# Two token blocks share the weight groups of the first MLP, and the weight steps are spread out

## The chip, the cores and the metric

The kernel runs on one core of one Trainium2 chip. The metric is device time in microseconds (us) of one execution. The engines are TensorE (PE in the profile, with its weight loads as PEld), VectorE (DVE), ScalarE (ACT), GpSimd (POOL) and SyncE (SP), whose queue issues all the DMAs here. A write "out<-in" in a row of the profile names the tiles that an instruction writes and reads; L785 is line 785 of the kernel before.

## The reference

Three layers in a row, float32 in and out, 4 batches of 576 tokens, 8 heads of 64:

```python
# 1 attention, with a decay by f
scores = scale * q @ k.T + (cum[:, None] - cum[None, :])    # cum = cumsum(log f), causal mask
attn = exp(scores - max) / (sum + 1e-9);  x = attn @ v      # -> x (2304, 512)
# 2 first MLP, w_in (512, 2048), w_out (2048, 512)
h = x @ w_in;  g = h * tanh(softplus(h));  x = g @ w_out
# 3 second MLP, w_in (512, 1024), w_out (1024, 512)
h = x @ w_in;  s = h * softmax(h);  z = layernorm(s) * g_ln;  out = z @ w_out
```

The weights come as float64 values.

## The kernel before

**Precision.** TensorE works on fp16 here. Each float32 operand is split into a high and a low fp16 half under a power-of-two scale, and each product is three matmuls (high·high, high·low, low·high).

**Attention** makes x in chunks of 128 tokens (64 in one chunk of each batch), in "slots" of four, two or one heads: 30 slots to a batch. A slot's scores go into one of three PSUM tiles `sp` (L436, L437, L441 on the PE). `step_r` takes the maximum on the DVE (L483; for a chunk of 64 tokens L493, L496 and L497) and the exponential on ACT (L485, or L499 and L500). `step_h` casts the high half (L523, ACT), subtracts for the low half (L524, POOL) and transposes both by a DMA on the SP queue (`pT`, L529). Three slots later L555 to L557 multiply by v. `fin` scales the chunk (L566 to L574) and transposes it by DMA (L582) into `xT`, blocks of 256 tokens, in three buffers.

**The weights of the first MLP** come in 16 parts of 1 MB, in four groups: group g holds two parts of w_in (`wi_r`) and two of w_out (`wo_r`), which serve the hidden tiles fi = 4g to 4g+3 of 128 channels. `load` (L121) issues a part's DMA on the SP queue into one of two buffers. `conv` (L130) turns float64 bits into float32 with three DVE steps (L137, L139, L141) and issues eight small matmuls (`gram`, L160), from which `bound` derives the scale of a group (L175 to L180, L329). `split` makes the halves, on ACT and POOL (L201, L203, L206) or on ACT and DVE (L198, L199). All these steps stand in one list, `wsteps`, and `wgo(n)` emits the next n. During the first slots WS0 = 3 are emitted a slot, and later WS1 = 4 in each half step of the loop below.

**The first MLP** goes block by block (j, nine blocks), in units of one fi: unit n is block n // 16, fi n % 16. `up` (L775) makes h for a pair of units in PSUM, 12 matmuls each (L785). `mish_a`, `mish_b` and `mish_c` make g (L797, L798 on ACT; L802 and L806 on DVE; L803 to L805 and L811 on ACT; L812 on POOL). `down` (L818) multiplies by w_out, 12 matmuls to a unit (L829). Block 0 closes its sum after each group of four fi and adds it, with the group's own scale `rho`, to `acc` in SBUF (L838 and L840 on the DVE), since the later groups' scales are not known yet; the other blocks sum all 16 fi in PSUM. `evac` (L847) hands the block to the second MLP, whose work (L1028, L1068) begins when attention is done.

**The order.** One loop of half steps (L906 to L954) writes the program: it emits the weight steps that a unit needs, and paces the attention slots through `att_slots` (L890), with EB = 190 half steps for all of them, a lower bound from the next block's need and an upper bound from the three `xT` buffers. A scheduler then fixes each engine's order from this program, so an engine's order can differ from the order of the lines.

Of the kernel before, what the change touches and what calls it, by code (L numbers as in the profile page):

```python
# [8 lines left out]
F32 = mybir.dt.float32  # L9
F16 = mybir.dt.float16  # L10
# [8 lines left out]
P = 128  # L19
# [18 lines left out]
R0 = 9  # L38
GRP = [4, 2, 1, 1, 1]
WS0 = 3  # L40
WS1 = 4
WPF = 2
S2P = 1
EB = 190
# [164 lines left out]
def emit(tc, q, k, v, f, w_in, w_out, w2_in, w2_out, g_ln, out):  # L209
# [580 lines left out]
    def mish_a(p):  # L790
        j, fi = divmod(2 * p, NF1)
        ph = hps.pop(p)
        ta = mp.tile([P, 2, TB], F32, tag="ta", name=f"ta_{p}")
        th = mp.tile([P, 2, TB], F32, tag="th", name=f"th_{p}")
        tmp[p] = (ta, th)
        for b, a, e in segs(j):
            nc.scalar.activation(ta[:, :, a:e], ph[:, :, a:e], AF.Exp, scale=usc(b, fi // 4))  # L797
        nc.scalar.activation(th, ph, AF.Copy, scale=ths[:, fi // 4:fi // 4 + 1] if j else -0.4 * HSC)  # L798

    def mish_b(p):  # L800
        ta, th = tmp[p]
# [16 lines left out]
    def down(n):  # L818
        j, fi = divmod(n, NF1)
        gt = gts[n // 2]  # L820
        if n % 2:
            del gts[n // 2]
        first, last = (fi % 4 == 0, fi % 4 == 3) if j == 0 else (fi == 0, fi == NF1 - 1)
        for t in range(TT):
            if first:
                x2ps[j, t] = psx.tile([P, DM], F32, tag=f"x2_{t}", name=f"x2_{j}_{t}_{fi}")
            o = x2ps[j, t]
            for m, (lg, lw) in enumerate(((0, 0), (0, 1), (1, 0))):
                nc.tensor.matmul(  # L829
                    o, gt[:, lg, n % 2, t * P:(t + 1) * P], wout[:, fi, lw * 512:(lw + 1) * 512],  # L830
                    start=(first and m == 0), stop=(last and m == 2))
        if last and j == 0:
            for t in range(TT):
                o = x2ps.pop((0, t))
                g = fi // 4
                if g == 0:
                    acc[t] = mp.tile([P, DM], F32, tag="acc", name=f"acc{t}")
                    nc.vector.tensor_scalar(acc[t], o, rho[:, g:g + 1], None, op0=ALU.mult)  # L838
                else:
                    nc.vector.scalar_tensor_tensor(acc[t], o, rho[:, g:g + 1], acc[t], op0=ALU.mult, op1=ALU.add)  # L840
                if g == 3:
                    x2ps[0, t] = acc[t]
        if fi == NF1 - 1:
            for t in range(TT):
                evac(j, t)

    def evac(j, t):  # L847
# [12 lines left out]
        for p0 in (0, 64):  # L860
            b = (tt * P + p0) // S
            if p0 and b == (tt * P) // S:
                continue
            if j == 0:
                if t == 0:
# [5 lines left out]
            nc.vector.scalar_tensor_tensor(  # L871
                us2[p0:, tt:tt + 1], m[p0:, 1:2], 2.0 ** -14, (kb[b] if j else kbz)[p0:], op0=ALU.mult, op1=ALU.mult)

    need = []
    for j in range(NBLK):
# [14 lines left out]
    def att_slots(n):  # L890
# [11 lines left out]
    wq = {}  # L902
    done = {"d": 0}
    st2 = None

    for hn in range(2 * (NF + 5)):  # L906
# [2 lines left out]
        att_now = live and pos["k"] < att_slots(hn)  # L909
        if att_now:  # L910
            slot_pre()
        if half == 0:
            if n % 2 == 0 and 0 <= n // 2 - 1 < NF // 2:
                mish_b(n // 2 - 1)
            if att_now:
                slot_mid()
            if live:
                while n < NF1 and (w1_split, n // 4 * 2 + 1) not in wdone:
                    wgo(1)
                up(n)  # L920
        else:
            if live and n % 2:
                while n > NF1 and wsteps:
                    wgo(1)
                mish_a(n // 2)
            if n % 2 == 0 and 0 <= n // 2 - 1 < NF // 2:
                mish_c(n // 2 - 1)
            if att_now:
                slot_mid()
            tgt = n - 2 if (n > DL + 8 or n >= NF) else n - DL  # L930
            while done["d"] < min(tgt, NF):
                if done["d"] // 2 not in gts:
                    break
                while done["d"] < NF1 and (w2_split, done["d"] // 2) not in wdone:
                    wgo(1)
                down(done["d"])
                done["d"] += 1
        if att_now:
            slot_pe()
# [180 lines left out]
```

## Time and profile before

| | us |
|---|---|
| median of 3 runs (lowest to highest) | 859.61 (858.01 to 860.01) |
| the profiled execution's own span, first to last instruction | 856.0 |
| busy in it: PE, DVE, ACT, POOL | 739.0, 617.6, 548.2, 440.8 |

The median stands 3.6 us above the span of the profiled execution; that is what lies around the span, plus the difference between runs. Busy time of matmuls is modelled where they are pipelined, so a PE that reads as 95% busy may be full. The profile's "PEclk" is the share of full TensorE speed that was granted. The share of the whole span hides that the stages differ: up to about 140 us the weights are still being converted, from then to about 500 us attention and the first MLP run together, and from 600 us on the chain of work that ended last is matmuls alone.

### The profile page before, as it was taken

What the parts mean: (1) busy time and instruction counts of PE and PEld (TensorE: products, weight loads), DVE (VectorE), ACT (ScalarE), POOL (GpSimd) and SP (SyncE); (2) the same over time, 40 slices, a digit from 0 to 9 for tenths busy, and PEclk for the clock granted to TensorE, in tenths of its full rate; (3) what the DMA queues carried; (4) which work ended last, traced back from release to release, by engine and by line L of the source; (5) the groups of instructions that cost most, each with busy time, mean ns of one, the idle gap of its engine ahead of it and who ended that gap; (6) DMA issues with size and microseconds to landing.
All of it is one profiled execution on the core that took longest, in us unless ns stands there. A gap on an engine that the chain in (4) does not pass through costs nothing.

```text
span 856.0 us, 15746 instructions
## 1 busy us (share of the span) xinstructions
PE 739.0 (86%) x5822; PEld 456.4 (53%) x5822; DVE 617.6 (72%) x1158; ACT 548.2 (64%) x1202; POOL 440.8 (51%) x341
## 2 busy tenths in 40 slices
PE   0545776689999999997999999986999999999998
PEld 0334543447656666575666767553555554444443
DVE  6799999498867989769896755599566444665551
ACT  5645647868779877877877767686855554333331
POOL 2268676755976667755678653128832222022110
PEclk9999997889999999999999999999999999999999
DMA  9999555477899898988897533941013323344443
GB/s 239 229 215 281 160 176 94 93 137 145 153 174 190 168 169 153 184 155 153 173 180 119 115 70 63 233 156 61 26 38 87 74 64 73 87 101 106 104 88 82
DMA packets 328568, 114.83 MB, mean 134 GB/s; under 512 B 317676, under 2 KB 317676, under 8 KB 328492
## 3 DMA queue, kind: packets, MB, share of 16 engines
q1 hardware_dynamic: 328492, 113.84, 63.9%
q8 instruction: 45, 0.74, 0.4%
q14 instruction: 31, 0.25, 0.1%
HBM read 46.59 MB, written 9.55 MB: 66 GB/s over the span
## 4 chain that ended last, share of the span: by engine, by line
PE 37%; DVE 24%; DMA 12%; ACT 11%; issue 8%; POOL 6%; SPq 1%; DVEq 0%; ACTq 0%; POOLq 0%
PE h L1028 11%; PE o L1068 10%; PE x L829 7%; PE h L785 6%; DMA pT<-ph 3%; POOL ph L524 3%; DVE th L806 2%; DVE ta L802 2%; ACT p L485 2%; DVE ph L521 1%; DMA w2i_r<-in_moe_w_in_dram 1%; DMA ktr<-kn 1%; DMA rawk<-in_k_dram 1%; ACT p L500 1%; DVE nm L483 1%
## 5 line engine op out<-in xcount | busy, mean ns | idle before, releaser
L829 PE MATMUL x<-wout,gt 128*128 128x512 f16 x864 | 219.8, 387 | 18.2 <-ACT gt L811 8.8
L785 PE MATMUL h<-xT,win 128*128 128x256 f16 x1728 | 221.2, 277 | 2.3 <-POOL win L203 1.7
L524 POOL TENSOR_TENSOR ph<-p,ph 128x512 f16<-128x512 f32 (+4 forms) x120 | 157.0, 1314 | 81.3 <-ACT ph L523 35.0
L785 PEld LDWEIGHTS <-win 128*128 128x128 f16 x1728 | 168.5, 100 | 45.8 <-POOL win L203 1.8
L812 POOL TENSOR_TENSOR gt<-th,gt 128x512 f16<-128x512 f32 x72 | 92.4, 1284 | 106.5 <-ACT gt L811 105.3
L829 PEld LDWEIGHTS <-gt 128*128 128x128 f16 x864 | 80.0, 100 | 99.3 <-ACT gt L811 11.6
L1056 POOL TENSOR_TENSOR z<-sl,z 128x1024 f16<-128x1024 f32 x18 | 38.7, 2151 | 138.0 <-DVE s2c L1035 111.1
L1028 PE MATMUL h<-w,x2T 128*128 128x512 f16 x432 | 98.4, 380 | 2.9 <-POOL w L206 1.6
L1068 PE MATMUL o<-wo,zT 128*128 128x512 f16 x432 | 96.5, 379 | 0.5 <-DMA zT<-z 0.5
L555 PE MATMUL pv<-vt,pT 128*128 128x64 f16 (+3 forms) x480 | 71.4, 203 | 23.0 <-DMA pT<-ph 20.2
L806 DVE SCALAR_TENSOR_TENSOR th<-ta,th 128x512 f32<-128x512 f32 x72 | 71.9, 1000 | 24.7 <-ACT ta L805 24.4
L485 ACT ACTIVATE p<-sp,nm 64x64 f32<-64x64 f32 (+7 forms) x128 | 61.3, 484 | 38.7 <-DVE nm L483 21.1
L436 PE MATMUL sp<-ktr,qa 128*128 128x64 f16 (+6 forms) x304 | 59.6, 253 | 22.8 <-ACT p L485 8.7
L811 ACT CAST gt<-th 128x512 f16<-128x512 f32 x72 | 44.3, 615 | 50.2 <-DVE th L806 49.9
L802 DVE TENSOR_SCALAR ta<-ta 128x512 f32<-128x512 f32 x72 | 58.8, 816 | 20.4 <-ACT ta L797 19.9
L1028 PEld LDWEIGHTS <-x2T 128*128 128x128 f16 x432 | 42.3, 98 | 53.9 <-issue 4.0
L555 PEld LDWEIGHTS <-pT 128*128 128x128 f16 (+3 forms) x480 | 45.4, 101 | 47.9 <-DMA pT<-ph 31.3
L556 PE MATMUL pv<-vt,pT 128*128 128x64 f16 (+3 forms) x480 | 70.4, 198 | 0.6 <-DVE vt L199 0.6
L557 PE MATMUL pv<-vt,pT 128*128 128x64 f16 (+3 forms) x480 | 70.2, 198 | 0.0
L1068 PEld LDWEIGHTS <-zT 128*128 128x128 f16 x432 | 42.2, 98 | 51.5 <-DMA zT<-z 1.0
L437 PE MATMUL sp<-ktr,qb 67*128 67x64 f16 (+6 forms) x304 | 63.3, 254 | 3.6 <-DVE qb L401 3.6
L1039 ACT ACTIVATE e<-h,s2c 128x1024 f32<-128x1024 f32 x18 | 21.7, 1204 | 68.1 <-DVE s2c L1037 68.1
(235 smaller groups left out, 1443.5 us busy)
## 6 DMA issues: line engine op xcount, KB each, us to landing
wi_r<-in_moe_w_in_dram SPq DMA_DIRECT2D x8, 1024.0 KB
wo_r<-in_moe_w_out_dram SPq DMA_DIRECT2D x8, 1024.0 KB
rawk<-in_k_dram SPq DMA_DIRECT2D x25, 256.0 KB
rawv<-in_v_dram SPq DMA_DIRECT2D x25, 256.0 KB
x2d<-x2h SPq DMA_DIRECT2D x18, 256.0 KB
out_dram<-ro SPq DMA_DIRECT2D x18, 256.0 KB
w2i_r<-in_moe_w_in_dram SPq DMA_DIRECT2D x4, 1024.0 KB
w2o_r<-in_moe_w_out_dram SPq DMA_DIRECT2D x4, 1024.0 KB
```

The lines of the kernel that those rows point to most:

```text
L485: nc.scalar.activation(pv[:m, g * (i + 1) * P + off:g * (i + 1) * P + end], s3[:, g, off:end], AF.Exp, bias=nm[:m, g:g + 1], accum_out=rs[ ...
L524: nc.gpsimd.tensor_tensor(p4[:, :, 1], pv3, p4[:, :, 0], op=ALU.subtract)
L555: nc.tensor.matmul(o, pT[a0:a1, k, :m], vh, start=(c == 0), stop=False)
L556: nc.tensor.matmul(o, pT[a0:a1, k, :m], vl, start=False, stop=False)
L557: nc.tensor.matmul(o, pT[a0:a1, k + 1, :m], vh, start=False, stop=(c == i))
L785: nc.tensor.matmul(ph, win[:, (fi // 4) * NC1 + c, col:col + P], x[:, lx * NC1 + c, :], start=(m == 0), stop=(m == 3 * NC1 - 1))
L802: nc.vector.tensor_scalar(ta, ta, E20, 1.0, op0=ALU.min, op1=ALU.add)
L806: nc.vector.scalar_tensor_tensor(th, ta, 2.5, th, op0=ALU.subtract, op1=ALU.mult)
L812: nc.gpsimd.tensor_tensor(gt[:, 1], th, gt[:, 0], op=ALU.subtract)
L829: nc.tensor.matmul(o, gt[:, lg, n % 2, t * P:(t + 1) * P], wout[:, fi, lw * 512:(lw + 1) * 512], start=(first and m == 0), stop=(last and ...
L1028: nc.tensor.matmul(h[:, half * 512:(half + 1) * 512], x[:, lx * NC1 + c, :], self.w2[:, half * NC1 + c, lw * 512:(lw + 1) * 512], start=(n ...
L1068: nc.tensor.matmul(o, zT[:, lz * NF2 + c, :], self.wo[:, c, lw * 512:(lw + 1) * 512], start=(n == 0), stop=(n == 3 * NF2 - 1))
```

## The change

- The order of units is a list: block 0's groups 0 (fi 0 to 3) and 1, then block 1's group 0, block 0's group 2, block 1's group 1, and so on, block 1 one group behind; from unit 28 on it is as before. So the first 32 units are 0–3, 4–7, 16–19, 8–11, 20–23, 12–15, 24–27, 28–31.
- Blocks 0 and 1 (j < NR = 2) both close their sums after each group. Block 1's `acc` lies in the third `xT` buffer, and its scales take the form that block 0's had (a constant at L798, `kbz` at L871).
- Weight steps are forced only by a unit that needs them; WS1 goes from 4 to 1 a half step.
- Until unit 15 is emitted, attention may not pass slot 32 (of 120).
- `across` (L329), which borrows a score tile of PSUM for a scale's sum, picks one that no pending score holds.

```diff
-WS1 = 4
+WS1 = 1
+NR = 2
...
-            k = seq[min(pos["k"], len(seq) - 1)]
-            t = sps[cnt["s"] % (len(sps) if k[1] < NCH - 1 else 2)]
-            cnt["s"] += 1
+            k = [seq[min(max(pos["k"] - x, 0), len(seq) - 1)][1] for x in range(2)]
+            held = [x[3].name for y, x in pend.items() if y[0] == "s"]
+            free = [x for x in sps[:len(sps) if max(k) < NCH - 1 else 2] if x.name not in held]
+            t = free[cnt["s"] % len(free)]
...
-        first, last = (fi % 4 == 0, fi % 4 == 3) if j == 0 else (fi == 0, fi == NF1 - 1)
+        first, last = (fi % 4 == 0, fi % 4 == 3) if j < NR else (fi == 0, fi == NF1 - 1)
...
                 if g == 0:
-                    acc[t] = mp.tile([P, DM], F32, tag="acc", name=f"acc{t}")
-                    nc.vector.tensor_scalar(acc[t], o, rho[:, g:g + 1], None, op0=ALU.mult)
+                    if j == 0:
+                        acc[j, t] = mp.tile([P, DM], F32, tag="acc", name=f"acc{t}")
+                    elif t == 0:
+                        w = mlpx.tile([P, 2 * NC1, TB], F16, tag="xT", name=f"xT_acc{j}", bufs=XB)
...
+                    nc.vector.tensor_scalar(acc[j, t], o, rho[:, g:g + 1], None, op0=ALU.mult)
...
         hi = need[j + XB] - 1 if j + XB < NBLK else len(seq) + LAG
+        if n < 2 * units.index(NF1 - 1):
+            hi = min(hi, sum(H // g for g in GRP) + LAG - 1)
...
+    units = list(range(0, 4))
+    for g in range(1, 4):
+        units += list(range(4 * g, 4 * g + 4)) + list(range(NF1 + 4 * g - 4, NF1 + 4 * g))
+    units += list(range(NF1 + 12, NF))
...
-                while n < NF1 and (w1_split, n // 4 * 2 + 1) not in wdone:
+                while u < NR * NF1 and (w1_split, u % NF1 // 4 * 2 + 1) not in wdone:
                     wgo(1)
-                up(n)
+                up(u)
```

What this moves on three engines follows; the lines of the changed kernel are one or two higher up to L830 and eight or nine higher up to L960.

**DVE around the end of the last group's conversions** (`wi_r7`, `wo_r6` are weight parts as they came; `nm_0_3_7` is the negative maximum of batch 0, chunk 3, head 7; `x2_0_0_4` is block 0's sum of group 1). Before, from the last step of `wi_r7` to the first of `wo_r6`:

```order
L141 SCALAR_TENSOR_TENSOR win_93<-wi_r7_758,win_93 128x1024
L179 RECIPROCAL wo_b_159<-wo_b_159 128x1
L628 TENSOR_TENSOR rho_90<-wpt_83,wo_b_159 128x1
L567 TENSOR_SCALAR rr_0_2_1071<-rsum_0_2_591 128x8
L180 TENSOR_SCALAR wo_b_159<-wo_b_159 128x1
L568 RECIPROCAL rr_0_2_1071<-rr_0_2_1071 128x8
L137 TENSOR_SCALAR wout_94<-wo_r6_820 128x1024
```

Now, the same stretch:

```order
L142 SCALAR_TENSOR_TENSOR win_93<-wi_r7_975,win_93 128x1024
L848 SCALAR_TENSOR_TENSOR acc0_1223<-x2_0_0_4_1340,rho_90,acc0_1223 128x512
L569 TENSOR_SCALAR rr_0_3_1387<-rsum_0_3_888 128x8
L848 SCALAR_TENSOR_TENSOR acc1_1225<-x2_0_1_4_1344,rho_90,acc1_1225 128x512
L570 RECIPROCAL rr_0_3_1387<-rr_0_3_1387 128x8
L495 TENSOR_REDUCE ne_0_1289<-sp2_149 64x8
L200 SCALAR_TENSOR_TENSOR wout_94<-wout_94,wo_b_159 128x2x512
L498 TENSOR_REDUCE nm_0_4_0_1288<-sp0_147 64x1
L498 TENSOR_REDUCE nm_0_4_1_1327<-sp1_148 64x1
L176 TENSOR_REDUCE wi_b_158<-gram_151 128x1
L499 TENSOR_TENSOR nm_0_4_0_1288<-nm_0_4_0_1288,ne_0_1289 64x1
L138 TENSOR_SCALAR wout_94<-wo_r6_1159 128x1024
```

Two of block 0's sums, the end of chunk 3, the first two heads of chunk 4 and a split stand there now; the heads 0 to 7 of chunk 3 stand further ahead, two of them directly before `wi_r7`.

**SP queue around the last weight loads** (`rawk`, `rawv`, `rawq` are loads of attention's inputs, `pT` the transposes of its probabilities, `qa` of its queries). Before:

```order
L124 DMA wo_r5_689<-in_moe_w_out_dram 128x2x512
L302 DMA rawk_1_3_1266<-in_k_dram 128x8x64
L124 DMA wi_r6_745<-in_moe_w_in_dram 128x2x512
L124 DMA wi_r7_758<-in_moe_w_in_dram 128x2x512
L124 DMA wo_r6_820<-in_moe_w_out_dram 128x2x512
L398 DMA_TRANSPOSE qa_0_4_1184<-qn_0_4_1180 128x8x64
L124 DMA wo_r7_870<-in_moe_w_out_dram 128x2x512
```

Now:

```order
L303 DMA rawq_1_0_1601<-in_q_dram 64x8x64
L303 DMA rawk_1_0_1603<-in_k_dram 64x8x64
L531 DMA_TRANSPOSE pT_0_3_0_930<-ph_0_3_0_892 128x16x128
L125 DMA wi_r7_975<-in_moe_w_in_dram 128x2x512
L303 DMA rawv_1_0_1605<-in_v_dram 64x8x64
L531 DMA_TRANSPOSE pT_0_3_2_1025<-ph_0_3_2_985 128x16x128
L531 DMA_TRANSPOSE pT_0_3_4_1120<-ph_0_3_4_1075 128x16x128
L125 DMA wo_r6_1159<-in_moe_w_out_dram 128x2x512
L531 DMA_TRANSPOSE pT_0_3_6_1215<-ph_0_3_6_1169 128x16x128
L125 DMA wo_r7_1285<-in_moe_w_out_dram 128x2x512
L531 DMA_TRANSPOSE pT_0_4_0_1338<-ph_0_4_0_1295 128x20x64
```

The load of `wi_r7` stands behind the transpose `pT_0_3_0`, and those of `wo_r6` and `wo_r7` behind three more of chunk 3, where before no transpose of probabilities stood between `wi_r6` and `wo_r7`.

**ACT after the last group's conversions** (`ta_9`, `th_9` belong to block 1's fi 2 and 3, `ta_4` to block 0's fi 8 and 9). Now:

```order
L502 ACTIVATE p32_1_130,rsum_0_4_1287<-sp1_148,nm_0_4_3_1618 64x512
L501 ACTIVATE p32_0_129,rsum_0_4_1287<-sp2_149,nm_0_4_4_1704 64x64
L502 ACTIVATE p32_0_129,rsum_0_4_1287<-sp0_147,nm_0_4_4_1704 64x512
L805 ACTIVATE ta_9_1540<-ta_9_1540 128x512
L202 ACTIVATE rawk_1_2_2161<-rawk_1_2_2161,scu_1_1357 128x512
L813 CAST gt_8_1512<-th_8_1472 128x512
L799 ACTIVATE ta_4_1607<-h_0_8_1557,usc1_0_79 128x512
```

Block 1's first pairs stand ahead of block 0's pair 4, which before stood ahead of chunk 3's exponentials, as here:

```order
L797 ACTIVATE ta_5_1541<-h_0_10_1505,usc1_0_79 128x512
L798 ACTIVATE th_5_1542<-h_0_10_1505 128x512
L198 ACTIVATE wout_94<-wout_94,wo_b_159 128x2x512
L811 CAST gt_4_1518<-th_4_1490 128x512
L803 ACTIVATE ta_5_1541<-ta_5_1541 128x512
L804 ACTIVATE ta_5_1541<-ta_5_1541,c_k1_72 128x512
L805 ACTIVATE ta_5_1541<-ta_5_1541 128x512
L485 ACTIVATE p32_0_129,rsum_0_3_1005<-sp0_147,nm_0_3_0_1006 128x512
```

## Rows read from the trace of the kernel before

**Rows 1.** The page, its 40 equal slices, busy tenths and TensorE clock.

```profile
PE   0545776689999999997999999986999999999998
...
PEclk9999997889999999999999999999999999999999
```

**Rows 2.** The table by stretch: window, length, then busy us (count) of each engine, clock.

```profile
98.00:140.50 42.50, 32.33 (x217) 19.16 (x215) 41.08 (x59) 24.40 (x40) 25.86 (x14) 0.88 0.48 127
140.50:200.00 59.50, 45.40 (x432) 29.17 (x431) 43.48 (x99) 47.41 (x112) 39.95 (x30) 0.86 0.67 131
200.00:289.30 89.30, 84.91 (x850) 57.68 (x849) 69.95 (x133) 73.32 (x182) 64.58 (x59) 1.00 0.92 163
289.30:400.00 110.70, 101.98 (x1059) 69.86 (x1057) 92.55 (x157) 87.65 (x220) 77.05 (x69) 1.00 0.93 167
600.00:856.00 256.00, 251.79 (x1297) 126.40 (x1294) 133.00 (x327) 113.35 (x210) 67.99 (x40) 1.00 0.35 78
```

**Rows 3.** The chain that ended last, two stretches of matmuls of one kind: start, us, what.

```profile
185.11 4.93 PE h L785 x28
...
611.31 2.62 PE h L785 x24
```

**Rows 4.** Waits of the PE in 140 to 200: us, times, longest us.

```profile
PE pv L555 <- DMA pT<-ph: 4.1, 3, 2.3
PE sp L436 <- ACT p L500: 4.1, 2, 3.3
PE sp L436 <- ACT p L485: 3.0, 3, 1.2
```

**Rows 5.** Timeline of the PE around 289: start, us, what.

```profile
289.15 0.71 PE L785 MATMUL h<-xT,win 128*128 128x256 f16 x5
```

**Rows 6.** Timeline of the DVE, last weight conversions and others: start, us, what.

```profile
125.51 0.71 DVE L137 TENSOR_SCALAR wout<-wo_r 128x1024 int32<-128x1024 int32 x1 [1.15 <-DMA wo_r<-in_moe_w_out_dram]
...
138.68 1.21 DVE L141 SCALAR_TENSOR_TENSOR wout<-wo_r,wout 128x1024 int32<-128x1024 int32 x1
```

**Rows 7.** Timeline of the DVE, one conversion step twice: start, us, what.

```profile
63.01 1.21 DVE L139 SCALAR_TENSOR_TENSOR win<-wi_r,win 128x1024 int32<-128x1024 int32 x1
...
82.89 3.02 DVE L139 SCALAR_TENSOR_TENSOR win<-wi_r,win 128x1024 int32<-128x1024 int32 x1
```

**Rows 8.** Groups by line on the DVE, 98 to 140: count, busy us, mean ns, idle.

```profile
L139 DVE SCALAR_TENSOR_TENSOR wout<-wo_r,wout 128x1024 int32<-128x1024 int32 x4 | 7.1, 1781 | 0.0
...
L806 DVE SCALAR_TENSOR_TENSOR th<-ta,th 128x512 f32<-128x512 f32 x5 | 5.1, 1025 | 0.0
...
L141 DVE SCALAR_TENSOR_TENSOR win<-wi_r,win 128x1024 int32<-128x1024 int32 x2 | 4.4, 2176 | 0.0
...
L802 DVE TENSOR_SCALAR ta<-ta 128x512 f32<-128x512 f32 x4 | 2.4, 611 | 0.0
...
L483 DVE TENSOR_REDUCE nm<-sp 128x1 f32<-128x512 f32 (+1 forms) x3 | 1.8, 633 | 0.0
...
L570 DVE TENSOR_TENSOR x<-pv,rr 128x512 f32<-128x512 f32 x1 | 0.7, 692 | 0.3 <-PE pv L557 0.3
...
L573 DVE CAST xh<-x 128x512 f16<-128x512 f32 x1 | 0.4, 409 | 0.0
...
L97 DVE TENSOR_SCALAR wi_b<-wi_b 128x1 int32<-128x1 int32 x2 | 0.3, 140 | 0.0
```

**Rows 9.** The same on the DVE, 140 to 200.

```profile
L496 DVE TENSOR_REDUCE nm<-sp 64x1 f32<-64x512 f32 x8 | 5.5, 682 | 5.1 <-PE sp L437 4.9
...
L840 DVE SCALAR_TENSOR_TENSOR acc<-x,rho,acc 128x512 f32<-128x512 f32 x4 | 2.9, 741 | 1.4 <-PE x L829 1.4
...
L497 DVE TENSOR_TENSOR nm<-nm,ne 64x1 f32<-64x1 f32 x8 | 2.4, 304 | 0.1
```

**Rows 10.** The same on ACT, 98 to 140.

```profile
L805 ACT ACTIVATE ta<-ta 128x512 f32<-128x512 f32 x5 | 3.1, 629 | 0.1
...
L485 ACT ACTIVATE p<-sp,nm 128x512 f32<-128x512 f32 (+1 forms) x3 | 1.9, 650 | 8.1 <-DVE nm L483 8.1
L523 ACT CAST ph<-p 128x512 f16<-128x512 f32 (+1 forms) x3 | 1.6, 584 | 0.0
```

**Rows 11.** Timeline of the SP queue, 110 to 142: start, us, what.

```profile
119.46 0.37 SPq L124 DMA_DIRECT2D wo_r<-in_moe_w_out_dram  x1
```

**Rows 12.** Waits of the SP queue, 40 to 200: us, times, longest us.

```profile
SPq L529 <- POOL ph L524: 15.4, 7, 5.9
```

More of the change, by code (lines that the diff above doesn't have):

```diff
@@ L831, in down @@
                     start=(first and m == 0), stop=(last and m == 2))
[L832 removed]
+        if last and j < NR:
             for t in range(TT):
[L834 removed]
+                o = x2ps.pop((j, t))
                 g = fi // 4
                 if g == 0:
[L837 to L840 removed]
+                    if j == 0:
+                        acc[j, t] = mp.tile([P, DM], F32, tag="acc", name=f"acc{t}")
+                    elif t == 0:
+                        w = mlpx.tile([P, 2 * NC1, TB], F16, tag="xT", name=f"xT_acc{j}", bufs=XB)
+                        w = w.rearrange("p c t -> p (c t)").bitcast(F32).rearrange("p (t e) -> p t e", t=TT)
+                        for x in range(TT):
+                            acc[j, x] = w[:, x]
+                    nc.vector.tensor_scalar(acc[j, t], o, rho[:, g:g + 1], None, op0=ALU.mult)
+                else:
+                    nc.vector.scalar_tensor_tensor(
+                        acc[j, t], o, rho[:, g:g + 1], acc[j, t], op0=ALU.mult, op1=ALU.add)
                 if g == 3:
[L842 removed]
+                    x2ps[j, t] = acc[j, t]
         if fi == NF1 - 1:
@@ L863, in evac @@
                 continue
-            if j == 0:
-                if t == 0:
+            if j < NR:
+                if tt == 0:
                     nc.vector.tensor_scalar(kbz, iv[0], 2.0 ** -28 / HSC, None, op0=ALU.mult)
@@ L898, in att_slots @@
         hi = need[j + XB] - 1 if j + XB < NBLK else len(seq) + LAG
+        if n < 2 * units.index(NF1 - 1):
+            hi = min(hi, sum(H // g for g in GRP) + LAG - 1)
         return min(max(x, lo), hi)
     NF = NBLK * NF1
-    wq = {}
+    units = list(range(0, 4))
+    for g in range(1, 4):
+        units += list(range(4 * g, 4 * g + 4)) + list(range(NF1 + 4 * g - 4, NF1 + 4 * g))
+    units += list(range(NF1 + 12, NF))
+    pairs = [u // 2 for u in units[::2]]
     done = {"d": 0}
@@ L911, in emit @@
             slot_pre()
+        u = units[n] if live else None
+        prev = pairs[n // 2 - 1] if n % 2 == 0 and 0 <= n // 2 - 1 < NF // 2 else None
         if half == 0:
-            if n % 2 == 0 and 0 <= n // 2 - 1 < NF // 2:
-                mish_b(n // 2 - 1)
+            if prev is not None:
+                mish_b(prev)
             if att_now:
@@ L917, in emit @@
             if live:
-                while n < NF1 and (w1_split, n // 4 * 2 + 1) not in wdone:
+                while u < NR * NF1 and (w1_split, u % NF1 // 4 * 2 + 1) not in wdone:
                     wgo(1)
-                up(n)
+                up(u)
         else:
             if live and n % 2:
-                while n > NF1 and wsteps:
+                while u >= NR * NF1 and wsteps:
                     wgo(1)
-                mish_a(n // 2)
-            if n % 2 == 0 and 0 <= n // 2 - 1 < NF // 2:
-                mish_c(n // 2 - 1)
+                mish_a(u // 2)
+            if prev is not None:
+                mish_c(prev)
             if att_now:
@@ L931, in emit @@
             while done["d"] < min(tgt, NF):
-                if done["d"] // 2 not in gts:
+                d = units[done["d"]]
+                if d // 2 not in gts:
                     break
-                while done["d"] < NF1 and (w2_split, done["d"] // 2) not in wdone:
+                while d < NR * NF1 and (w2_split, d % NF1 // 2) not in wdone:
                     wgo(1)
-                down(done["d"])
+                down(d)
                 done["d"] += 1
```

4 lines of the change are left out of this document (2 added, 2 removed).

## The prediction, made before the run

> **What bounds the kernel now.** I read the page's slices first. In them the PE is full from slice 9 on and thin before, and its clock drops below full speed only in slices 4 to 8 [rows 1]. The last 256 us are 98% PE, and the PE keeps 92% in 289 to 400 [rows 2], so time can only be won before about 290 us, or by taking matmuls away, which the change doesn't do.
>
> Then the table by stretch [rows 2]. In 98 to 140.5 the DVE is busy 41.08 of 42.5 us: it is the bound there, and the last of its weight conversions, at 138.68 + 1.21 = 139.9 us [rows 6], ends that stage. In 140.5 to 200 no engine is full: PE 45.40 of 59.5, DVE 43.48, ACT 47.41 (80%), POOL 39.95, so the PE stands idle for 14.1 us. The waits name what ended its idle time: exponentials that free a score tile (4.1 and 3.0 us) and transposed probabilities (4.1 us) [rows 4]. Those are waits of attention; the MLP has no work to put into them, because block 1 begins only when all of block 0 is done. The clock is 0.86 there. The chain shows the price of the lower of its two levels: block 1's first 28 matmuls take 4.93 us, 176 ns each, against 2.62 us for 24, 109 ns each, at full speed [rows 3]. In 200 to 289.3 the PE is busy 95%, with the clock at 1.00 [rows 2].
>
> Two marks carry the sum. **A** is the end of the last weight conversion, 139.9 us. **B** is 289.3 us, where block 2's fi 12 begins [rows 5]: the PE has done the same work by that place in both orders, and from there on the two orders are essentially the same. What the change does must show in B.
>
> **The change part by part.**
>
> *Up to A, the DVE.* Since it is 97% busy, what is put ahead of its last conversion moves A by its full length. In the order of the DVE these now stand ahead of it and stood behind it before: six maxima of chunk 3 (6 × 0.633), three of chunk 4 with their second steps (3 × 0.682 + 3 × 0.304), one more reduce of scores like them (0.68), the scaling and cast of chunk 3 (0.692 + 0.409), two reciprocal steps and five small ones of batch 1's scales (7 × 0.14 = 1.0) [rows 8, 9]. That is 3.8 + 2.05 + 0.91 + 0.68 + 1.1 + 1.0 = 9.5 us. Gone from ahead of it are two L802 and one L806 of block 0's pairs 4 and 5: 2 × 0.611 + 1.025 = 2.25 [rows 8]. A moves by +7.3, to 147.2.
>
> *Up to A, the SP queue.* The load of `wi_r7` now waits behind the transpose `pT_0_3_0`, which waits for a low half on POOL, which stands behind four split steps of the weight group before. A load takes 6.05 us from its issue at 119.46 [rows 11] to the conversion that waits for it at 125.51 [rows 6]. If the DVE runs dry for all of it, A moves by 6.05; if the load is still early enough, by 0. The transposes of that stretch already wait 15.4 us for POOL, 5.9 at most [rows 12], but the DVE itself lost only 1.15 us to a load [rows 6]. I take 1.2, with both ends kept.
>
> *Up to A, POOL beside the DVE.* Eight more low-half subtracts of POOL now stand ahead of the last group's split. The same conversion step took 1.21 us and, at another place, 3.02 [rows 7]. In 98 to 140 the steps of L139 and L141 averaged 1.78 and 2.18 us [rows 8] with 14 POOL instructions beside them [rows 2]: against 1.21, four times 0.57 and twice 0.97 is 4.2 us in those two rows, about 0.3 for each POOL instruction. Eight more cost 2.4 at that rate; the bounds are 0 and four meetings at the full 1.81, 7.2. I take 2.4. The Trainium skill bears on this (page "SBUF — State Buffer", section "Who interferes with whom"): a DVE instruction with two SBUF inputs and a GpSimd instruction that reads SBUF block each other, and "issue order, not op shape, decides who blocks". The trace agrees as far as 1.21 against 3.02 goes. By that rule each meeting may cost a whole POOL instruction, and the sum would go to the upper bound; it speaks against a change that lays attention's subtracts beside the conversions.
>
> A: 147.2 + 1.2 + 2.4 = 150.8 us, between 147 and 160.
>
> *Block 1's own sums.* Four groups by two tiles are eight more DVE instructions at 0.741 [rows 9], 5.9 us. They fall behind A, where the DVE is 73 to 84% busy [rows 2], so most of it lies in its gaps; as load it is counted in the next step. If that cover is gone it costs 5.9. The third `xT` buffer that the sums occupy is not wanted while attention is capped at slot 32, so I price it, the cap and the choice of score tile at nothing: ahead of the cap lies all of batch 0, and what hides them is that block 0 and 1's matmuls are there to run; without that cover the nearest row is a wait for a score tile, 3.3 us [rows 4].
>
> *From A to B.* Before, 149.4 us, with DVE 43.48 + 69.95 = 113.4 us busy (76%), ACT 47.41 + 73.32 = 120.7 (81%), PE 130.3 (88%) [rows 2]. The DVE's load there becomes 113.4 + 5.9 − 9.5 + 2.25 = 112.1. ACT's falls likewise: nine heads' exponentials and casts go ahead of A, 9 × (0.650 + 0.584) = 11.1, and about one pair's six ACT steps at some 0.63 come back, 3.8 [rows 10]: 113.4. The PE's own work from A to B is equal in both, but it now has two blocks to choose from as soon as the weights are there, so the idle 14.1 us and the low clock of 140.5 to 200 should shrink. How dense can it be? ACT reached 82% in 200 to 289.3 and DVE 84% in 289.3 to 400 [rows 2]; these are the best mixed stretches. With 83% for the two, 113 / 0.83 = 136 us; at 80% (ACT's share in 140.5 to 200) it is 141, at 85% it is 133.
>
> B: 150.8 + 136 = 286.8 us, against 289.3: −2.5. With the median as base, since everything behind B and what lies around the span (859.61 − 856.0 = 3.6) stays, 859.6 − 2.5 = **857.1 us**. So a delay of 10.9 us at A is paid back with 13.4 behind it. This case's own range is 852 (85%, A at 150) to 862 (80%, or A three later).
>
> **Rivals.**
>
> *The weights become late and it is slower.* If the load of `wi_r7` and its followers wait out the whole 6.05 us and four conversions meet a subtract at 1.81, A is 147.2 + 6.05 + 7.2 = 160.5, B 296.5, and the time 866.8. It decides from the point where A passes 289.3 − 136 = 153.3. For it: the transposes' waits on POOL already come to 15.4 us [rows 12], and POOL gets more. Against it: SP's longest single wait for POOL is 5.9, and the loads have two buffers. Chance 0.27.
>
> *The gain is larger.* If the added DVE work goes into places where it would have waited, so that A is 147, and the stretch reaches 87%, then 113 / 0.87 = 130, B 277, and 847. For it: the PE reached 95% as soon as two blocks' work was there [rows 2]. Against it: no stretch of before shows ACT or DVE above 84%. Chance 0.13.
>
> *Work only changes places.* The waits on exponentials and transposes [rows 4] are attention's own and stay; what is idle behind A moves ahead of it, and B stays at 289.3 within 2: 859.6. For it: the sum above is a difference of two terms over four times its size. Against it: 0.86 of the clock [rows 2] is a loss that denser matmuls take away. Chance 0.14.
>
> **How the numbers follow.** The forecast's case has 0.46. About 0.3% or 2.6 us is what a measurement of this kernel can tell from no change, so faster is below 857.0 and slower above 862.2. Of the forecast's case, 0.25 lies below 857.0 (its middle stands at that edge), 0.17 within and 0.04 above. Faster: 0.25 + 0.13 + 0.02 of the third rival = 0.40. Slower: 0.04 + 0.26 + 0.03 = 0.33; the slow rival keeps 0.01 inside. Same: 0.17 + 0.01 + 0.09 = 0.27. The range reaches to both outer cases, 846 to 868.
>
> **What the profile of the changed kernel will show.** The last L142 on the DVE should end near 151 us; under 147 the added work was hidden, above 154 the slow rival holds, and then the DVE rows `<-DMA wi_r` or a mean of the conversion steps above 2 us say which half of it. Behind it, block 1's first matmuls should begin within 5 us of the last conversion, not 45 us behind it as now (185.11 [rows 3]), and block 2's fi 12 should begin near 287. The clock in the 60 us behind A should be above 0.95; if it is still 0.86, the waits of attention were the limit and not the lack of matmuls. The forecast is wrong if block 2's fi 12 begins before 283 or after 292, or if the stretch behind it, 289 to 500 before, changes its length by more than 2 us, since I hold it to be the same.

## The result, and the profile after

The changed kernel takes 869.17 us (median of 4 runs, 867.85 to 872.76) against 858.95 for the kernel before in the same session: ratio 1.0125, interval 1.0101 to 1.015. It is slower by 10.2 us; the prediction said 857.1, and 869.17 lies just above its range (846 to 868).

The profiled execution (span 870.8 us) is the slowest of the four. Its first product with v of chunk 1 starts at 51.9 us instead of 49.7, at a place that both kernels' engines reach in the same order, so 2.2 of its 14.8 us belong to that execution and not to the change.

The page's slices of PE and clock, as [rows 1]:

```profile
PE   0446766789999997999998899976999999999998
...
PEclk9999876699999999999899999999999999999999
```

The clock falls to 8, 7, 6 and 6 tenths in slices 5 to 8, where [rows 1] has 7, 8 and 8 in slices 7 to 9. The table by stretch of the changed kernel, with the columns of [rows 2]:

```profile
98.00:140.50 42.50, 30.63 (x208) 17.23 (x208) 35.58 (x49) 29.70 (x61) 34.11 (x20) 0.80 0.72 163
140.50:200.00 59.50, 44.87 (x417) 31.65 (x414) 47.09 (x92) 40.03 (x90) 37.61 (x24) 0.80 0.58 117
200.00:289.30 89.30, 82.92 (x810) 55.89 (x810) 74.10 (x138) 68.96 (x169) 60.98 (x55) 1.00 0.82 148
159.10:219.10 60.00, 53.33 (x482) 37.49 (x483) 43.01 (x84) 49.52 (x114) 35.02 (x27) 0.94 0.57 95
```

The VectorE was 97% busy in 98 to 140.5 and is 84% busy now (35.58 of 42.5): the stage is no longer bound by its work. In 140.5 to 200 the PE is busy as long as before (44.87 against 45.40) but gets less done (417 matmuls against 432), at a clock of 0.80 instead of 0.86. The last line is the 60 us behind the last conversion. What the VectorE waits for stands in its timeline (start, us, what, and in brackets the idle time before it):

```profile
127.53 0.16 DVE L340 TENSOR_REDUCE sctkv<-st 128x2 f32<-128x10 f32 x1 [1.39 <-ACT jkv L317]
...
133.26 0.69 DVE L485 TENSOR_REDUCE nm<-sp 128x1 f32<-128x512 f32 x1 [2.20 <-PE sp L443]
135.40 0.69 DVE L485 TENSOR_REDUCE nm<-sp 128x1 f32<-128x512 f32 x1 [1.44 <-ACT p L487]
137.15 0.69 DVE L138 TENSOR_SCALAR win<-wi_r 128x1024 int32<-128x1024 int32 x1 [1.07 <-DMA wi_r<-in_moe_w_in_dram]
137.88 3.02 DVE L140 SCALAR_TENSOR_TENSOR win<-wi_r,win 128x1024 int32<-128x1024 int32 x1
...
157.16 1.92 DVE L142 SCALAR_TENSOR_TENSOR wout<-wo_r,wout 128x1024 int32<-128x1024 int32 x1
```

From 125.5 to 137.2 us it idles six times, 6.7 us in all, before the first step of `wi_r7`. Only 1.07 us of it stand as a wait for the load itself; the rest are waits of the steps ahead of it in the VectorE's order, most of them attention's. The last conversion ends at 157.16 + 1.92 = 159.1 us, not at 139.9 [rows 6]. The SP queue of that time:

```profile
125.78 0.60 SPq L303 DMA_DIRECT2D rawk<-in_k_dram  x1
128.68 1.88 SPq L531 DMA_TRANSPOSE pT<-ph  x1
130.65 1.03 SPq L125 DMA_DIRECT2D wi_r<-in_moe_w_in_dram  x1
131.78 0.61 SPq L303 DMA_DIRECT2D rawv<-in_v_dram  x1
132.79 7.47 SPq L531 DMA_TRANSPOSE pT<-ph  x2
140.31 0.58 SPq L125 DMA_DIRECT2D wo_r<-in_moe_w_out_dram  x1
```

The load of `wi_r7` was issued at 130.65, behind the transpose at 128.68; the next one, of `wo_r6`, at 140.31, behind 7.47 us of two transposes. In [rows 11] that load went out at 119.46.

Block 1's first matmuls follow the last conversion by 4.2 us:

```profile
163.27 4.37 PE L787 MATMUL h<-xT,win 128*128 128x256 f16 x24
```

Block 2's fi 12 begins at 297.6 us (289.3 in [rows 5]). So from the last conversion to it the kernel needs 138.5 us where it needed 149.4; the forecast was 136. But then the rest is longer too. The two stretches from block 2's fi 12 to the first product with v of attention's last chunk, before and after:

```profile
289.30:493.90 204.60, 189.26 (x1971) 130.70 (x1968) 168.79 (x292) 157.38 (x390) 143.90 (x130) 0.99 0.85 156
```

```profile
297.60:508.60 211.00, 192.10 (x1972) 132.75 (x1969) 162.75 (x292) 157.52 (x389) 145.91 (x131) 0.98 0.88 154
```

204.6 us before, 211.0 now: 3.6 us more idle time of the PE and 2.8 more busy time, in a stretch that the prediction held to be the same.

**A mark that moves with the end.** In all 20 profiled kernels of this study (before, changed, e1 to e18) the span ends 359.6 to 363.4 us after attention's last chunk starts its first product with v. That start moves between 491.5 and 519.6 us. The end of the weights moves between 138 and 173 us, and goes little with the span (correlation 0.2; 0.4 without e1). The mark is a place in the whole order and not attention's alone: ahead of it the PE has also done the `up` matmuls of 89 to 92 of the 144 units, in every kernel. So it shows that the time is lost ahead of it, and does not show that attention is what loses it. Times in us, from each kernel's timeline:

| kernel | last weight matmul ends | batch 1's first product | block 2, fi 12 | last chunk's first product | span |
|---|---|---|---|---|---|
| before | 140.6 | 209.2 | 289.3 | 493.9 | 856.0 |
| changed | 162.6 | 218.4 | 297.6 | 508.6 | 870.8 |
| e1, shared order, 4 steps | 139.5 | 231.5 | 312.7 | 519.6 | 879.2 |
| e2, old order, 1 step | 156.8 | 203.6 | 289.4 | 491.5 | 854.0 |
| e10, tile choice alone | 138.2 | 211.7 | 299.4 | 508.0 | 870.1 |
| e12, 1 step, tile in rotation | 154.6 | 193.0 | 296.6 | 496.8 | 858.1 |
| e18, e12 and own sums | 156.5 | 195.9 | 295.7 | 504.2 | 867.6 |
| e13, changed, tile in rotation | 161.2 | 210.4 | 291.0 | 500.2 | 862.5 |
| e16, before, pace 188 | 144.7 | 209.8 | 291.4 | 502.0 | 864.6 |

### The profile page after: what moved, and what is told of

The parts are those of the page before. It is cut to its first block, busy times and chain, and to the rows that moved or that the text cites. A ratio compares the mean times of both kernels' runs of the same rounds, so it can differ in the third digit from the quotient of the medians.

```text
span 870.8 us, 15762 instructions
## 1 busy us (share of the span) xinstructions
PE 745.3 (86%) x5822; PEld 462.1 (53%) x5822; DVE 619.8 (71%) x1166; ACT 548.0 (63%) x1202; POOL 445.4 (51%) x341
## 4 chain that ended last, share of the span: by engine, by line
PE 33%; DVE 25%; DMA 16%; ACT 10%; issue 9%; POOL 6%; SPq 1%; DVEq 0%; POOLq 0%; ACTq 0%
PE h L1046 10%; PE o L1086 10%; DMA pT<-ph 6%; PE x L831 5%; PE h L787 5%; POOL ph L526 4%; DVE ta L804 3%; DVE th L808 2%; DMA ktr<-kn 2%; DMA wi_r<-in_moe_w_in_dram 2%; DMA w2i_r<-in_moe_w_in_dram 1%; ACT p L487 1%; DMA rawv<-in_v_dram 1%; ACT ta L806 1%; DVE win L140 1%
## 5 line engine op out<-in xcount | busy, mean ns | idle before, releaser
L526 POOL TENSOR_TENSOR ph<-p,ph 128x512 f16<-128x512 f32 (+4 forms) x120 | 164.1, 1375 | 71.3 <-DVE ph L523 27.0
L557 PE MATMUL pv<-vt,pT 128*128 128x64 f16 (+3 forms) x480 | 72.8, 205 | 23.6 <-DMA pT<-ph 20.7
L805 ACT ACTIVATE ta<-ta 128x512 f32<-128x512 f32 x72 | 45.3, 631 | 46.7 <-DVE ta L804 46.7
L558 PE MATMUL pv<-vt,pT 128*128 128x64 f16 (+3 forms) x480 | 71.7, 201 | 0.6 <-DVE vt L200 0.6
L559 PE MATMUL pv<-vt,pT 128*128 128x64 f16 (+3 forms) x480 | 71.6, 201 | 0.0
L439 PE MATMUL sp<-ktr,qb 67*128 67x64 f16 (+6 forms) x304 | 65.3, 259 | 4.7 <-DMA ktr<-dd 3.0
```

The costliest lines, as they stand in the source:

```text
L526: nc.gpsimd.tensor_tensor(p4[:, :, 1], pv3, p4[:, :, 0], op=ALU.subtract)
L557: nc.tensor.matmul(o, pT[a0:a1, k, :m], vh, start=(c == 0), stop=False)
L558: nc.tensor.matmul(o, pT[a0:a1, k, :m], vl, start=False, stop=False)
L559: nc.tensor.matmul(o, pT[a0:a1, k + 1, :m], vh, start=False, stop=(c == i))
```

## The experiments

The kernel before ran beside each group of runs with a median of 859.2 to 860.3; times below are medians.

**e1 to e4: is the late end of the weights the loss?**

e1, in the changed kernel:

```diff
-WS1 = 1
+WS1 = 4
```

> The changed kernel with four weight steps a half step again, as before; the shared weight groups, block 1's own sums and the cap stay. Theory 1 (the weight steps, spread out, made the last conversion late, and that is the loss): the last conversion ends near 140 us instead of 159, and since the shared groups shorten the way from the last weight matmuls to block 2's fi 12 (135.0 us in the changed kernel, 148.7 before), that mark comes near 276 to 280 and the time is 847 to 853. Rival (the way is shorter only because attention's work was moved ahead of the last conversion; nothing is won by sharing): the way grows back to about 147 and the time is 857 to 861. Rival 2 (the shared order itself costs): above 863.

Measured: 882.99 (ratio 1.0268, 1.0239 to 1.0297), the slowest of all, with the weights as early as before (139.5 us). Theory 1 and the first rival failed; the second said no more than above 863. The PE in e1's table and timeline:

```profile
98.00:140.50 42.50, 25.47 (x185) 14.84 (x185) 40.55 (x63) 21.36 (x37) 27.06 (x15) 0.81 0.53 146
140.50:200.00 59.50, 41.25 (x348) 26.27 (x349) 30.20 (x69) 43.12 (x101) 33.48 (x26) 0.65 0.67 118
```

```profile
145.13 0.58 PE L438 MATMUL sp<-ktr,qa 128*128 128x512 f16 x1 [2.82 <-ACT p L487]
...
152.62 0.58 PE L438 MATMUL sp<-ktr,qa 128*128 128x512 f16 x1 [5.41 <-ACT p L487]
...
181.31 6.03 PE L787 MATMUL h<-xT,win 128*128 128x256 f16 x48
```

With four steps the weights stand ahead of attention's slots, and chunk 3, which makes block 1's tokens, comes after them. The shared order puts block 1's group 0 ahead of block 0's group 2, so both stand behind chunk 3 in the PE's order, whose scores wait for exponentials (2.82 and 5.41 us). No matmul of either begins until 181.31, 42 us behind the last weight matmul; the stretch has a clock of 0.65. In the shared order, four steps a half step cost 13.8 us against one.

e2, in the kernel before (`WS1 = 4` to `WS1 = 1`):

> The kernel before with one weight step a half step and nothing else of the change. Theory 1: the last conversion becomes late by 14 to 20 us as in the changed kernel, and without shared groups the way behind it is shortened by the moved attention work alone, some 6 us: time 867 to 873. Rival (the delay is made by the shared order, in which block 1's work stands ahead): last conversion within 5 us of before, time 858 to 863.

Measured: 853.78 (0.9927, 0.9901 to 0.9953), with the last weight matmul 16 us later than before; theory 1 had that delay, but neither it nor the rival had the time. In this kernel a scale's sum takes a score tile whose scores are still held, so some probabilities come from overwritten scores; the time is that of a kernel which lacks this wait. It shows that 16 us at the end of the weights need not cost anything.

e3, in the changed kernel:

```diff
-        if self.after is not None and self.after():
+        if self.after is not None and self.after() and n < 6:
```

> The changed kernel, but the loads of the last four weight parts are no longer tied behind the latest transpose of probabilities on the SP queue. Theory 1a (the load of wi_r7, which was issued at 130.65 us behind a transpose, starved the VectorE: 6.7 us of idle time between 125.5 and 137.2 us): the last conversion comes 6 to 9 us earlier, at 150 to 153, and the time falls by as much as 7, to 861 to 865. Rival (the attention work ahead of the conversions is the whole delay): the last conversion moves by under 3 us and the time stays at 867 to 871.

Measured: 865.87 (1.0073, 1.0045 to 1.0101). The load goes out early and its conversion starts without a wait; SP queue and VectorE of e3:

```profile
112.53 0.37 SPq L125 DMA_DIRECT2D wi_r<-in_moe_w_in_dram  x1
```

```profile
123.55 2.62 DVE L138 TENSOR_SCALAR win<-wi_r 128x1024 int32<-128x1024 int32 x1
```

The last conversion ends at 147.7 us, 11.4 earlier than in the changed kernel; block 2's fi 12 comes no earlier (299.0 against 297.6), and the time is 3.3 us shorter: theory 1a holds on where the VectorE waited, not on what the wait is worth.

e4, in the changed kernel:

```diff
-    for g in range(1, 4):
-        units += list(range(4 * g, 4 * g + 4)) + list(range(NF1 + 4 * g - 4, NF1 + 4 * g))
-    units += list(range(NF1 + 12, NF))
+    units = list(range(NF))
```

> The changed kernel with the units in their old order (block 0 whole, then block 1); the spread weight steps, block 1's own sums and the cap stay. Theory 1: the last conversion is as late as in the changed kernel or later, and without sharing the way behind it is not shortened by more than the moved work: 872 to 880. Rival (sharing wins nothing): 867 to 871, as the changed kernel. Against the run of the kernel before with one step a half step, the difference is the price of block 1's own sums: up to 6 us if nothing hides them, 0 if the gaps of the VectorE do.

Measured: 875.75 (1.018, 1.0136 to 1.0225). Without sharing it is 6.6 slower than the changed kernel: in this pair sharing wins, as the forecast had it, and something else loses more.

**e5 to e7: the cap, or block 1's own sums?**

e5 takes these lines out of the changed kernel; e6 and e7 do so too and have the old order of units, e6 with `NR = 1`:

```diff
-        if n < 2 * units.index(NF1 - 1):
-            hi = min(hi, sum(H // g for g in GRP) + LAG - 1)
```

> The changed kernel without the cap that holds attention at slot 32 until unit 15 is emitted. Theory 2 (attention sets the time: in six profiled kernels so far its last chunk starts 360 to 363 us ahead of the end; the cap makes batch 1 start 7 to 9 us late and nothing gives it back): batch 1's first product with v comes at 203 to 211 us instead of 218.4, attention's last at 494 to 500 instead of 508.6, and the time is 854 to 861. Rival (the late weights or the shared order delay attention, and the cap only writes down what would happen anyway): the marks move by under 3 us and the time stays at 866 to 870.

Measured: 872.38 (1.0151, 1.011 to 1.0191). Theory 2 fell: batch 1 started earlier (213.8), the last chunk did not (509.5). The time lies above the rival's 866 to 870 too.

> Of the change only the one weight step a half step and the choice of score tile in across; old order of units, no sums of block 1's own, no cap. Theory 2: attention is not held, so its last chunk starts at 490 to 495 us and the time is 852 to 856, as in the kernel before with one step a half step (853.8), though the last conversion is 10 us or more later than before. Rival (that time came from the score tile that a scale's sum took while its scores were still held): 859 to 863.

Measured: 864.34 (1.0059, 1.0039 to 1.0078): the rival, 10.6 above e2.

> As the run with one weight step and the choice of score tile, and besides block 1's own sums of each group (eight more VectorE instructions, and the third xT buffer for them); old order of units, no cap. The prediction's price of the sums is 0 to 5.9 us: theory 2 says 0 to 3 on top of the run without them. Rival (the buffer is the price: block 2's tokens of attention must wait for it, and the transposes that wait hold the SP queue): 8 us or more on top, as with the cap.

Measured: 875.59 (1.0194, 1.0167 to 1.022), 11.3 above e6, the rival's size. Block 1 (its first matmul to block 2's) and the two blocks behind it, in e6 and then in e7:

```profile
182.70:252.70 70.00, 65.00 (x653) 43.72 (x652) 51.57 (x95) 57.92 (x147) 48.43 (x41) 1.00 0.74 138
252.70:388.90 136.20, 128.14 (x1306) 87.23 (x1305) 104.38 (x196) 108.84 (x271) 93.45 (x85) 0.97 0.89 167
```

```profile
184.00:259.40 75.40, 68.59 (x634) 44.99 (x634) 56.79 (x101) 58.42 (x148) 48.86 (x43) 0.93 0.68 124
259.40:399.80 140.40, 128.98 (x1298) 88.06 (x1296) 104.09 (x199) 109.89 (x273) 96.06 (x83) 0.96 0.90 164
```

Block 1 takes 75.4 us instead of 70.0 with 5.2 us more of VectorE work, at a clock of 0.93; the next two blocks take 4.2 more.

**e8, e9: the sums or their buffer?** e8 puts e7's sums into the tiles that block 0's leave; e9 adds to e6 a hold of the third `xT` buffer:

```diff
 # e8
...
-                        w = mlpx.tile([P, 2 * NC1, TB], F16, tag="xT", name=f"xT_acc{j}", bufs=XB)
...
+                        acc[j, t] = mp.tile([P, DM], F32, tag="acc", name=f"acc{j}_{t}")
 # e9, in down, at fi 3 and fi 15 of block 1
+            hold = mlpx.tile([P, 2 * NC1, TB], F16, tag="xT", name="xT_hold", bufs=XB)
+            holds.append(hold)
+            nc.vector.memset(hold[:, 0, 0:1], 0.0)
...
+            nc.vector.memset(holds[0][:, 0, 0:1], 1.0)
```

> One weight step a half step, old order of units, no cap, and block 1's own sums, but in the tiles that block 0's sums leave behind, so that all three xT buffers stay with attention. Without own sums this is 864.3, with sums in the third xT buffer 875.6. Theory 3 (the eight sums are not hidden: the VectorE's time in that stage is on attention's path): 869 to 872, at least the 5.9 us of the eight instructions. Rival (the buffer is the price): 863 to 866.

Measured: 871.77 (1.0155, 1.0125 to 1.0186), 7.4 above e6.

> The same without own sums, but the third xT buffer is taken from block 1's first group to its last by two tiny memsets. Theory 3: 863 to 867. Rival (the buffer is the price, block 2's and block 3's tokens wait for buffers): 872 to 877. If both this run and the one with the sums alone lie between, the two prices add up.

Measured: 866.11 (1.01, 1.0073 to 1.0128), 1.8 above e6. In these runs the sums, not the buffer, carry most of it.

**e10 to e15: the choice of score tile, and the loads.** e10 is the kernel before with the new `across` alone; e11 is e6 with e3's edit.

> Of the change only the choice of score tile in across; four weight steps, old order. I priced it at nothing: 858 to 861. Rival (it orders the scales' sums behind scores and costs by itself, as between the two runs with one weight step, 853.8 and 864.3): 865 to 871.

Measured: 869.77 (1.0142, 1.0119 to 1.0165): an edit priced at nothing costs, alone, as much as the whole change. The new rule does not move the rotation on, so the next scores can go into the sum's own tile and wait until the VectorE has read it; the PE in e10:

```profile
126.24 0.38 PE L331 MATMUL sp<-wi_b,ones 128*128 128x1 f32 x2 [1.16 <-DVE wi_b L176]
129.05 0.59 PE L438 MATMUL sp<-ktr,qa 128*128 128x512 f16 x1 [2.42 <-DVE wi_b L178]
```

> One weight step a half step with the choice of score tile (864.3), and the loads of the last four parts not tied behind the latest transpose of probabilities. There the VectorE waited 5.3 us for wi_r7's load. Theory 1a (the late load is what this choice of tile cost): 855 to 860, so it may pass the kernel before. Rival (the wait is hidden by attention's own pace): 862 to 866.

Measured: 861.22 (1.0032, 1.0019 to 1.0044), 3.1 below e6, and not below the kernel before.

For e12 to e15 the sum takes the next tile of the rotation that is not held, and moves the rotation on:

```diff
-            free = [x for x in sps[:len(sps) if max(k) < NCH - 1 else 2] if x.name not in held]
-            t = free[cnt["s"] % len(free)]
+            nt = len(sps) if max(k) < NCH - 1 else 2
+            while sps[cnt["s"] % nt].name in held:
+                cnt["s"] += 1
+            t = sps[cnt["s"] % nt]
+            cnt["s"] += 1
```

> One weight step a half step, old order of units, and for a scale's sum the tile that is next in the rotation (passing over held ones) with the rotation moved on, as the kernel before does, so that the next scores go into another tile. With four weight steps this rule gives the kernel before, instruction for instruction. Theory 4 (the changed choice costs because the next scores land in the tile that the sum still occupies; 869.8 against 859.5 with four steps): 852 to 857 instead of 864.3, so the spread weight steps alone gain 3 to 7. Rival (only a held tile, overwritten, made the first run with one step fast): 862 to 866.

Measured: 860.42 (1.0016, 1.0 to 1.0032), between theory and rival: the rotation gives 3.9 back.

> The whole changed kernel with only this choice of tile put back into the rotation. Theory 4 (the parts add up: choice of tile +10.3, own sums with their buffer +11.3, spread steps -5.5, shared order -6.6): 857 to 862, about level with the kernel before. Rival (in the shared order the choice of tile does not matter, the loss is the own sums and the late weights): 866 to 870.

Measured: 864.38 (1.0066, 1.0041 to 1.0091), 4.8 below the changed kernel. The parts do not add up to theory 4's sum.

> As the changed kernel with the tile from the rotation, and the loads of the last four weight parts not tied behind the latest transpose (worth 3.3 in the changed kernel): theory 4 says 853 to 859. Rival: 863 to 867.

Measured: 865.91 (1.0077, 1.0061 to 1.0092), 1.5 above e13.

> One weight step a half step, tile from the rotation, loads of the last four parts free, nothing else of the change: the version to which the parts point. Theory 4: 849 to 855, faster than both kernels. Rival (with the tile from the rotation wi_r7's load is no longer late, so freeing it gives nothing): as the run with the tile from the rotation, within 2.

Measured: 866.74 (1.0086, 1.0071 to 1.0101), 6.3 above e12. Free loads gained 3 in two kernels and lost 1.5 and 6.3 in two others: their price belongs to the order, not to the loads.

**e16 to e18: what a mere reshuffle costs.** In the kernel before, `EB = 190` becomes 188 and 192; e18 is e7 with the tile from the rotation.

> The kernel before with EB = 188 instead of 190: attention is paced 1% faster, nothing else. It measures how far the time moves when every engine's order is reshuffled without any part of the change. Theory 4: within 2.6 us of before, so single parts of 3 us or more can be trusted. Rival (the order by itself is worth several us): 4 to 10 us off.

Measured: 868.12 (1.0097, 1.0073 to 1.0121).

> The same with EB = 192, 1% slower. Theory 4: within 2.6 us of before. Rival: 4 to 10 us off.

Measured: 865.26 (1.0053, 1.0026 to 1.008). Both reshuffles cost, 7.8 and 5.0 us: the rival. In e16 block 2's fi 12 is only 2.1 us late, but from there to the last chunk's first product it takes 210.6 us where the kernel before takes 204.6:

```profile
291.40:502.00 210.60, 192.31 (x1950) 131.85 (x1948) 163.32 (x291) 155.46 (x389) 143.47 (x130) 0.95 0.82 151
```

So this stretch lengthens by 6 us with no part of the change in it, as it does by 6.4 in the changed kernel.

> Block 1's own sums in the third xT buffer, on top of one weight step and the tile from the rotation (860.4), old order of units, no cap. If the price of the sums and the buffer is theirs and not the order's, it repeats: 869 to 874. Rival (the 11.3 of the first pair of runs was a matter of order): 861 to 866.

Measured: 870.61 (1.0135, 1.0105 to 1.0164), 10.2 above e12: the price of the own sums repeats. Its place does not: e7 loses 5.4 us within block 1, e18 nothing there and 10.8 in the two blocks behind it.

**Idle, or slower?** The stretch from the first `up` matmul to the last chunk's first product holds nearly the same matmuls in every kernel. Its lines, with the columns of [rows 2], for before, changed, e16, e6, e7, e12 and e18:

```profile
76.60:493.90 417.30, 365.88 (x3585) 247.74 (x3582) 344.52 (x602) 314.11 (x739) 291.29 (x238) 0.96 0.80 155
79.50:508.60 429.10, 370.28 (x3578) 252.40 (x3576) 345.44 (x609) 312.67 (x736) 296.25 (x238) 0.93 0.80 150
77.30:502.00 424.70, 372.72 (x3569) 251.08 (x3566) 337.67 (x601) 313.95 (x741) 293.56 (x238) 0.94 0.79 152
77.90:500.10 422.20, 366.38 (x3577) 246.37 (x3576) 339.51 (x600) 312.71 (x739) 296.20 (x239) 0.95 0.78 153
77.50:513.90 436.40, 372.68 (x3577) 251.16 (x3574) 343.53 (x608) 313.56 (x738) 298.98 (x238) 0.93 0.76 148
77.90:496.80 418.90, 363.77 (x3576) 247.36 (x3573) 341.65 (x601) 314.49 (x741) 294.17 (x239) 0.96 0.80 154
80.20:504.20 424.00, 371.90 (x3576) 252.62 (x3574) 345.89 (x607) 311.20 (x735) 295.29 (x238) 0.93 0.77 152
```

The length less the PE's busy time is its idle time. e16 idles as long as the kernel before (52.0 us, 51.4) but is busy 6.8 us longer. e18 idles 3.0 us less than e12 and is busy 8.1 longer. e7 against e6 has 7.9 more idle and 6.3 more busy, the changed kernel against before 7.4 and 4.4. In all four the mean clock is lower by 0.02 to 0.03. So in e16 and e18 the time went into longer matmuls, at a lower mean clock, and not into waits; in the other two it went into both. What makes the clock fall more often in these orders was not tested, and by itself it does not order the kernels: e10 has a mean clock of 0.975 over its span of 870.1 us, e2 0.962 over 854.0.

**The runs by group.** Without own sums and in the old order of units, eight edited kernels (e6, e9 to e12, e15 to e17; e2, with its overwritten scores, is left out) lie at 860.4 to 869.8, mean 865.2. With own sums, old order, four (e4, which also has the cap, e7, e8, e18): 870.6 to 875.8, mean 873.4. With own sums, shared order and one step, five (the changed kernel, e3, e5, e13, e14): 864.4 to 872.4, mean 867.5. Against edited kernels the own sums cost 8.2 and sharing gives 5.9 back; the kernel before, at 859.2, is itself 6.0 better than the mean of the eight. No version here beats it on a full computation.

## Why the prediction was wrong, point by point

- **The end of the weights.** Forecast 150.8 us, measured 159.1, or 156.9 without the late start of that execution. The term that was mis-sized is the SP queue's, taken at 1.2 us: in e3, with the loads free, the last conversion ends at 147.7, 11.4 us earlier and close to the 147.2 that the sum has without its queue and POOL terms. The slow rival named the right place, the load behind a transpose, and its numbers came near (160.5, block 2's fi 12 at 296.5, time 866.8). But as a price that is luck: it charged the delay to the end in full, and e3 has the weights 11.4 us earlier with fi 12 at 299.0; e1 and e2 also show that the end hardly follows this mark. POOL beside the VectorE was sized well: from `wi_r7` on, three of nine conversion steps were stretched (3.02, 2.06 and 1.92 us against 1.21), 3.4 us in all, forecast 2.4. By the Trainium skill (page "SBUF — State Buffer", section "Who interferes with whom") a VectorE instruction with two SBUF inputs contends with a GpSimd instruction that reads SBUF, and issue order decides who blocks; the trace agrees for the step of 3.02, which started at 137.88 beside a GpSimd subtract of 2.62 us started at 137.21. The full 1.81 us was lost once, not four times.
- **From the weights to block 2's fi 12.** The number came, 138.5 us, forecast 136, before 149.4, but the reason given for it is not shown. From the last conversion to this mark e2 and e6, which share nothing, need 133.3 and 125.9 us, and e3, which shares, 151.3: where the conversions end late, more of the other work already lies ahead of them. Block 1's matmuls came 4.2 us behind the last conversion, as forecast (within 5). Sharing is worth 6.6 us with the cap (e4) and 3.2 without it (e5 against e7), no more than a reshuffle. The clock in the 60 us behind the last conversion is 0.94, where the forecast said above 0.95 and the kernel before has 0.86.
- **Block 1's own sums.** This is the step that failed most. The sums were counted as load only, since "most of it lies in its gaps", and of the buffer the prediction says "I price it, the cap and the choice of score tile at nothing". The sums with their buffer cost 11.3 and 10.2 us in two settings, 7.4 without the buffer, for 5.9 us of instructions. They took what a row of before says, 0.74 us each:

```profile
L848 DVE SCALAR_TENSOR_TENSOR xT_acc<-x,rho,xT_acc 128x512 f32<-128x512 f32 x6 | 4.2, 738 | 0.0
...
L846 DVE TENSOR_SCALAR xT_acc<-x,rho 128x512 f32<-128x512 f32 x2 | 1.5, 742 | 0.0
```

  The gaps were there, 16 to 27% of the VectorE, and yet even the "5.9" of a lost cover was too low in all three pairs, though each pair also carries a reshuffle's 5 to 8 us. A sum stands in one queue with attention's maxima, but that it delays the end by them is not shown: the time is lost at different places in e7 and e18, and in e18 as longer matmuls with less idle time. How the sums reach the end, by a wait or by the clock, stays open.
- **The choice of score tile.** Also priced at nothing; it costs 4.8 us within the changed kernel (e13), 3.9 between e12 and e6, and 10.6 alone (e10). Its wait, 2.42 us of the PE on the VectorE's read of a scale's sum, was to be seen in the code: the rotation no longer moves on. How much of the 10.6 is such waits and how much the reshuffle stays open.
- **Everything behind block 2's fi 12 "stays".** The tiles are the same there, but scores and products with v fall between the MLP's matmuls in another order up to 493 us, and the stretch grew by 6.4 us. e16 shows that a new order alone can do that (6.0); others shorten it, to 198.8 us in e11. The kernel before stands at a pace at which two steps either way cost 5 to 8 us. I forecast a gain of 2.5 from a sum that held that order fixed. Both of the prediction's own signs of being wrong came: fi 12 after 292, and this stretch changed by more than 2.
- **Smaller slips.** The clock of the kernel before falls in slices 7 to 9 of [rows 1], not 4 to 8. The 176 ns of block 1's first matmuls are no price of the lower level: the mean clock in 185.11 to 190.04 us is 0.64, so they mix both levels. And 85% with A at 150 gives 853 us, not 852. None of these moves the forecast.
- **The account.** A chain of runs, each with one edit more: before 859.2; one step and rotation, e12, 860.4 (+1.2); own sums, e18, 870.6 (+10.2); shared order and cap, e13, 864.4 (-6.2); new choice of tile, changed kernel, 869.2 (+4.8). In another chain (e10, e6, e7, e5, changed) the same parts read +10.6, -5.4, +11.3, -3.2 and, for the cap, -3.2. Signs agree for tile, sums and sharing, not for the spread steps. Only the own sums, and the tile in e10, come to more than the 7.8 us of a neutral reshuffle, so the other sizes are uncertain.

## What to carry to other kernels

Look for the mark that moves with the end over several variants (here attention's last chunk, 360 to 363 us ahead of the end) before an earlier mark is charged to the total; and count what all engines have done by then before one chain is named for it. Idle time on an engine is no reason to price added work at nothing: here eight instructions of 5.9 us, on a VectorE that was 73 to 84% busy, came with 7.4 to 11.3 us. Split a loss on the PE into idle time and busy time for the same matmuls, with the granted clock beside it, before a wait is looked for. Where a scheduler orders everything, run two neutral edits of the kernel before: their spread (here 5 to 8 us, 0.5 to 1.0%) is the least that a single edit's price can mean.

## What the runs showed that was not expected

The same tuned program, paced 1% faster or slower, lost 7.8 and 5.0 us, where the runs of the kernel before lie within 2 to 5 us of each other in a session: its speed hangs on its exact pace and order. And weights that ended as early as before (139.5 us in e1) went with the slowest kernel, 883.0, because its order let the PE's queue stand behind the attention chunk that the shared blocks need first.
